# Linear attention and two MLPs on one core: seven block products in place of eight in the second MLP's first layer, and the first MLP two chunks at a time

## The chip, the cores and the metric

The kernel runs on one core of a Trainium2 chip. Times are device microseconds (us); shorter is better. Engines are named as in the profile: PE is TensorE (PEld are its weight loads), DVE VectorE, ACT ScalarE, POOL GpSimd, SP the engine that issues most DMAs.

## The reference

Three parts follow each other. `x` of the attention goes to the first MLP, whose output goes to the second one; `x` has 1152 tokens (2 batches of 576) of 512 features.

```
def phi(x):
    proj = np.einsum('bhsd,df->bhsf', x, w_phi)
    proj = proj - np.max(np.abs(proj), axis=-1, keepdims=True)
    return np.concatenate([np.exp(proj), np.exp(-proj)], axis=-1)
q_p, k_p = (phi(q), phi(k))
num = np.einsum('bhsf,bhfd->bhsd', q_p, np.einsum('bhsf,bhsd->bhfd', k_p, v))
den = np.einsum('bhsf,bhf->bhs', q_p, np.sum(k_p, axis=2))[..., None] + 1e-06
x = (num / den)                     # 2 x 8 heads x 576 x 64, reordered to 1152 x 512
x = (x @ w_a) * (x @ w_b) @ w_out   # 512 -> 1536 -> 512
for e in range(4):                  # p: domain_probs, normed over the 4 experts
    out += p[:, e:e + 1] * (np.maximum(x @ w1[e], 0.0) @ w2[e])   # 512 -> 1024 -> 512
```

## The kernel before

Every value that a matmul of the MLPs reads is held as a high and a low part, each of a rounded 32-bit type (fp32r), and a product of two such values is three matmuls: high weights with high and low data, low weights with high data. High parts are copies on ScalarE, low parts subtractions on VectorE or GpSimd. The weights of the first MLP arrive as 64-bit words (`raw`) and are turned into 32-bit ones on the chip in three stages that lie apart: `words` (two ScalarE operations), `from_words` (three VectorE operations and one addition `wx` on GpSimd, L344) and `parts` (L375, L376).

The attention runs as a pipeline of 36 slots (18 for keys, 18 for queries; `NI` = 36, `NK` = 18) and some slots behind, in which the last divisions are made: `stage_x` on VectorE, and `stage_xparts`, which copies x to its high part (`xh`, L289) and makes the low part (`xl`, L290, GpSimd), a pair of heads at a time, in two pieces, since a batch is 576 tokens and a block 384. In the slots of `FILL` the first products of the first MLP are issued.

In the MLPs all data lie transposed, features on partitions, tokens in columns, in three blocks of 384 tokens (`TB`). Weights stand still in the array, a block's tokens stream. The hidden features come in chunks of 128.

- First MLP: `stage_ab` makes one chunk of one block, `a` and `b` (12 matmuls each), their product `gg` (L417) and its two parts `hh`. `stage_o1` adds the chunk to four tiles of PSUM (`acc`, 12 matmuls); after six chunks (`GF`) these are copied into `part` (L442), and the second six are added to that (L449); the result's two parts (L450, L451) are the second MLP's input.
- Second MLP: `stage_h` makes a chunk of an expert for a block (12 matmuls of 384 columns, L465 to L467), `hh` by relu and a subtraction (L472, L473), `stage_o2` adds it to three row tiles of 128 tokens (9 matmuls of 512 columns, L483 to L485). Per expert and block, eight chunks accumulate in PSUM, then `o2_sum` adds the row tiles, weighed by the tokens' probabilities, to `oacc`.

The order is a list `prog` by hand: the second layer of a chunk is issued after the first layer of the next one. `ahead` splits weights ahead of their use at one half per stage. All engines run their queues in the order of the program.

Of the kernel before, what the change touches and what calls it, by code (L numbers as in the profile page):

```python
# [38 lines left out]

@with_exitstack  # L40
def tile_linear_attention_then_mlps(ctx, tc, qT, kT, v, w_phi, wab, wout, w12, probs, out):
# [6 lines left out]
    wb = const.tile([128, 2, 128], F32, name="wb")  # L48
    wbp = const.tile([128, 2, 256], F32R, name="wbp")
# [4 lines left out]
    w1_p = tc.alloc_tile_pool(name="w1", bufs=1, side="left")  # L54
    k_p = tc.alloc_tile_pool(name="k", bufs=1, side="left")
    r_p = tc.alloc_tile_pool(name="r", bufs=1, side="right")
    q_p = None
    nd_p = tc.alloc_tile_pool(name="nd", bufs=2, space=PSUM)

    with tc.manual_schedule():  # L60
# [4 lines left out]
        # the table of exponentials is loaded while the first inputs are on their way  # L65
# [39 lines left out]
        def load_v(b, st):  # L105
            """Pairs of heads with a block of ones between the two."""
# [85 lines left out]

        def stage_kvz(b, p):
# [5 lines left out]
            t = r_p.tile([128, 2, 2, 128], F32, tag="kvz", name="kvz", bufs=B * NP)  # L199
# [39 lines left out]

        xh, xl = {}, {}  # L240

        def pieces(b):
            lo, end = b * S, (b + 1) * S
            while lo < end:
                tb = lo // TB
                hi = min(end, (tb + 1) * TB)
                yield tb, lo - tb * TB, hi - lo, lo - b * S
                lo = hi

        def stage_num(b, p):  # L250
# [3 lines left out]
            for h in range(2):  # L254
                t = nd_p.tile([128, 2, 512], F32, tag="nd", name="num")
                nd.append(t)
                for i in range(2):
                    for s in range(2):
                        nc.tensor.matmul(
                            out=t[:, i, 0:288], lhsT=kvz[:, h, s, :],  # L260
                            rhs=qp[:, s, h, 288 * i:288 * i + 288],
                            start=(s == 0), stop=(s == 1),
                        )
            den = q_p.tile([128, 2, 288], F32, tag="den", name="den", bufs=2)
            x = q_p.tile([128, 2, 288], F32, tag="x", name="x", bufs=3)
            for h in range(2):
                lo = 64 * h
                nc.scalar.activation(
                    out=den[lo:lo + 64], in_=nd[h][64 - lo:128 - lo, :, 0:288], func=AF.Copy, bias=1e-6
                )  # L270
                nc.scalar.activation(out=x[lo:lo + 64], in_=nd[h][lo:lo + 64, :, 0:288], func=AF.Copy)
            return x, den

        def stage_x(b, p, x, den):
# [5 lines left out]
            rb = q_p.tile([128, 2, 288], F32, tag="rb", name="rb", bufs=1)  # L280
            nc.vector.transpose(out=rb.rearrange("p a b -> p (a b)"), in_=dt.rearrange("p a b -> p (a b)"))
            nc.vector.tensor_tensor(out=x, in0=x, in1=rb, op=ALU.mult)
            return x

        def stage_xparts(b, p, x):
            xf = x.rearrange("p a b -> p (a b)")
            for tb, o, n, s in pieces(b):
                hi = xh[tb][:, p, o:o + n]
                nc.scalar.activation(out=hi, in_=xf[:, s:s + n], func=AF.Copy)  # L289
                nc.gpsimd.tensor_tensor(  # L290
                    out=xl[tb][:, p, o:o + n], in0=xf[:, s:s + n], in1=hi.bitcast(F32), op=ALU.subtract
                )

# [1 line left out]
        w2_p = None  # L295
        w_t = {}
        units = [("ab", f) for f in range(NF)] + [("o", 0), ("ab", 3), ("o", 1), ("ab", 4), ("ab", 5), ("o", 2)]
        units += [u for f in range(GF, FA) for u in [("ab", f)] + ([("o", f // 2)] if f % 2 == 0 else [])]
        units += [("e", n) for n in range(E * FE)]
        srcs = {"ab": wab, "o": wout, "e": w12}  # L300
# [416 lines left out]
```

## Time and profile before

| | |
|---|---|
| runs | 746.52, 746.54, 747.3 us (median 746.54) |
| span of the profiled execution, first to last instruction | 745.0 us, and some 1.5 us around it |
| PE busy | 734.0 us (99%), 3920 matmuls |
| DVE, ACT, POOL busy | 335.4, 268.3, 120.7 us |

The attention takes the first 126 us; then come the first MLP to about 340 us, and the second to 740. "Busy" of PE is the time that any matmul is in flight. A time in a list of instructions is one instruction's own duration; behind it, in brackets, stands how long its engine was idle before, and which instruction ended that.

### The profile page before, as it was taken

To read this page: it belongs to the slowest core of one execution; us is meant where nothing else is said; L and a number is where in the kernel's file an instruction comes from. 1 tells how busy PE (TensorE), PEld (TensorE's weight loads), DVE (VectorE), ACT (ScalarE), POOL (GpSimd) and SP (SyncE) were. 2 spreads that over 40 slices of the span, in tenths; PEclk is the share of its full clock that TensorE was granted. 3 is DMA by queue.
4 is the path that set the end of the run, shared out by engine and by line. 5 is a ranking of instruction groups with operands and counts; after the bars stand their busy time and mean duration, and the time that the engine had idled before them with its cause. 6 is when DMAs were issued, how large, how long until landed. Compare 5 with 4: busy or idle time off the path is not lost.

```text
span 745.0 us, 9704 instructions
## 1 busy us (share of the span) xinstructions
PE 734.0 (99%) x3920; PEld 680.9 (91%) x3920; DVE 335.4 (45%) x553; ACT 268.3 (36%) x546; POOL 120.7 (16%) x114
## 2 busy tenths in 40 slices
PE   7999999999999999999999999999999999999997
PEld 6888889999999999999999898999999899999996
DVE  6987988888179421336122441214332124222131
ACT  5877997566157221334111321112311114121110
POOL 3663436444034120202000000000000000000000
PEclk9999999999999999999999999999999999999999
DMA  7742011344034100023000330001300003001011
GB/s 233 219 129 76 1 38 70 126 163 143 1 107 148 57 0 1 1 86 116 26 1 1 113 113 1 1 0 59 140 29 0 1 16 127 0 1 43 0 44 44
DMA packets 20334, 46.07 MB, mean 62 GB/s; under 512 B 4592, under 2 KB 9136, under 8 KB 20288
## 3 DMA queue, kind: packets, MB, share of 16 engines
q1 hardware_dynamic: 20032, 45.25, 18.4%
q8 instruction: 31, 0.51, 0.3%
q10 hardware_dynamic: 224, 0.16, 0.1%
q14 instruction: 15, 0.12, 0.1%
q0 software_dynamic: 32, 0.03, 0.0%
HBM read 43.08 MB, written 2.36 MB: 61 GB/s over the span
## 4 chain that ended last, share of the span: by engine, by line
PE 87%; DVE 8%; ACT 2%; issue 2%; DMA 0%; DVEq 0%; POOL 0%; POOLq 0%
PE h L465 9%; PE h L467 9%; PE acc L485 9%; PE h L466 9%; PE acc L484 9%; PE acc L483 9%; PE ab L412 5%; PE ab L413 5%; PE ab L411 5%; PE kv L179 4%; PE acc L434 3%; PE acc L435 3%; PE acc L436 3%; DVE m L335 1%; PE pj L148 1%
## 5 line engine op out<-in xcount | busy, mean ns | idle before, releaser
L473 DVE SCALAR_TENSOR_TENSOR hh<-h,hh 128x384 fp32r<-128x384 f32 x96 | 53.6, 559 | 274.6 <-ACT hh L472 274.6
L472 ACT ACTIVATE hh<-h 128x384 fp32r<-128x384 f32 x96 | 47.1, 491 | 310.1 <-PE h L467 310.1
L465 PE MATMUL h<-xh,w 128*128 128x384 f32 x384 | 129.6, 338 | 0.0
L467 PE MATMUL h<-xh,w 128*128 128x384 f32 x384 | 129.6, 338 | 0.0
L466 PE MATMUL h<-xl,w 128*128 128x384 f32 x384 | 128.9, 336 | 0.0
L485 PE MATMUL acc<-w,hh 128*128 128x512 f32 x288 | 114.1, 396 | 0.0
L484 PE MATMUL acc<-w,hh 128*128 128x512 f32 x288 | 113.3, 393 | 0.0
L483 PE MATMUL acc<-w,hh 128*128 128x512 f32 x288 | 113.2, 393 | 0.0
L411 PE MATMUL ab<-xh,w 128*128 128x384 f32 x288 | 96.7, 336 | 0.0
L412 PE MATMUL ab<-xl,w 128*128 128x384 f32 x288 | 96.4, 335 | 0.3 <-POOL xl L290 0.3
L413 PE MATMUL ab<-xh,w 128*128 128x384 f32 x288 | 96.3, 334 | 0.0
L466 PEld LDWEIGHTS h<-xl,w 128*128 128x128 f32 x384 | 72.1, 188 | 3.9
L465 PEld LDWEIGHTS h<-xh,w 128*128 128x128 f32 x384 | 72.1, 188 | 3.8
L467 PEld LDWEIGHTS h<-xh,w 128*128 128x128 f32 x384 | 72.0, 188 | 0.0
L344 POOL TENSOR_TENSOR wx<-wx,rn 128x512 uint32<-128x512 uint32 x36 | 54.6, 1516 | 87.3 <-DVE wx L341 47.0
L485 PEld LDWEIGHTS acc<-w,hh 128*128 128x128 f32 x288 | 54.1, 188 | 12.5
L483 PEld LDWEIGHTS acc<-w,hh 128*128 128x128 f32 x288 | 54.5, 189 | 8.8
L484 PEld LDWEIGHTS acc<-w,hh 128*128 128x128 f32 x288 | 54.1, 188 | 8.9
L412 PEld LDWEIGHTS ab<-xl,w 128*128 128x128 f32 x288 | 54.1, 188 | 0.7 <-POOL xl L290 0.6
L411 PEld LDWEIGHTS ab<-xh,w 128*128 128x128 f32 x288 | 54.1, 188 | 0.1
L413 PEld LDWEIGHTS ab<-xh,w 128*128 128x128 f32 x288 | 54.0, 188 | 0.0
L417 DVE TENSOR_TENSOR gg<-ab,a 128x384 f32<-128x384 f32 x36 | 19.9, 554 | 73.7 <-PE ab L413 72.3
(78 smaller groups left out, 1067.5 us busy)
## 6 DMA issues: line engine op xcount, KB each, us to landing
raw<-in_w SPq DMA_DIRECT2D x32, 512.0 KB, 3.5
raw<-in_wab SPq DMA_DIRECT2D x24, 512.0 KB, 3.6
raw<-in_wout SPq DMA_DIRECT2D x12, 512.0 KB, 3.4
xraw<-in_qT SPq DMA_DIRECT2D x6, 384.0 KB, 3.0
out<-oacc SPq DMA_DIRECT2D x8, 256.0 KB, 2.0
xraw<-in_kT SPq DMA_DIRECT2D x5, 384.0 KB, 3.2
v<-in_v SPq DMA_DIRECT2D x8, 192.0 KB, 3.9
v<-in_v SPq DMA_DIRECT2D x8, 64.0 KB, 3.7
```

Of the source, the lines that this page charges most:

```text
L344: nc.gpsimd.tensor_tensor(out=x, in0=x, in1=r, op=ALU.add)
L411: nc.tensor.matmul(out=t, lhsT=whi, rhs=xh[tb][:, c, :], start=(c == 0), stop=False)
L412: nc.tensor.matmul(out=t, lhsT=whi, rhs=xl[tb][:, c, :], start=False, stop=False)
L413: nc.tensor.matmul(out=t, lhsT=wlo, rhs=xh[tb][:, c, :], start=False, stop=(c == KD - 1))
L465: nc.tensor.matmul(out=t, lhsT=whi, rhs=xh[tb][:, c, :], start=(c == 0), stop=False)
L466: nc.tensor.matmul(out=t, lhsT=whi, rhs=xl[tb][:, c, :], start=False, stop=False)
L467: nc.tensor.matmul(out=t, lhsT=wlo, rhs=xh[tb][:, c, :], start=False, stop=(c == KD - 1))
L472: nc.scalar.activation(out=hh[:, 0, :], in_=t, func=AF.Relu)
L473: nc.vector.scalar_tensor_tensor(out=hh[:, 1, :], in0=t, scalar=0.0, in1=hh[:, 0, :].bitcast(F32), op0=ALU.max, op1=ALU.subtract)
L483: nc.tensor.matmul(out=acc, lhsT=hi, rhs=whi, start=(f == 0), stop=False)
L484: nc.tensor.matmul(out=acc, lhsT=hi, rhs=wlo, start=False, stop=False)
L485: nc.tensor.matmul(out=acc, lhsT=lo, rhs=whi, start=False, stop=(f == FE - 1))
```

## The change

1. The first layer of the second MLP takes two chunks of an expert (256 hidden features, `j`, 16 pairs) and one batch of 576 tokens (`tp`) at a time. Its product is seen as 2 x 2 blocks: 256 of the 512 input features by 128 hidden features on one side, 256 features by 288 tokens (`HT`) on the other. Instead of the eight products of blocks, Strassen's seven are made (in Winograd's form), `M1` to `M7`: each is a sum or difference of weight blocks times one of data blocks, 6 matmuls of 288 columns. Products that are added to each other do so in PSUM (`X`, `Y`, `Z`) or in `c` in SBUF.
2. The sums of weight blocks (`sums_w`, tile `wt`, GpSimd, L409) and their two parts (`wc`), and the differences of data blocks (`sums_x`, tile `t`, GpSimd, L306) and their parts (`xc`, L83 and L84) are new; data are made once for each batch, weights once for each pair of chunks.
3. The second layer of that MLP is done for each pair of chunks and each of nine row tiles (6 matmuls of 512 columns), and each such tile is added to `oacc` at once (L646, L651): 16 x 9 sums where there were 4 x 9.
4. The first MLP takes two chunks and a batch at a time (`unit_ab`: eight steps of 12 matmuls of 288 columns; `o1`: eight pieces of 6 matmuls). The second layer's pieces are added to `part` in SBUF by VectorE (L497) each time.
5. The order comes from a queue: `run` issues a step of the first layer and after it pieces of the second that were queued three or more steps ago, at a rate; `tasks` is the list of the weights' preparations, `prep(1)` issues one of them after each step. Before a hidden tile `hhb`, of which there is now one for a batch, is written again, `free_hh` issues all pieces that read it. The last unit of the first MLP runs its pieces at twice the rate; after the first unit of the second MLP the queue is emptied.
6. x's parts lie by batch and are made in one piece of 576 columns. `FILL` has a slot more, with two steps in each.

The core of the diff, with what is new and called:

```diff
-        xh, xl = {}, {}
-        def pieces(b):
...
         def stage_xparts(b, p, x):
             xf = x.rearrange("p a b -> p (a b)")
-            for tb, o, n, s in pieces(b):
-                hi = xh[tb][:, p, o:o + n]
...
+            hi = xh[b][:, p]
+            nc.scalar.activation(out=hi, in_=xf, func=AF.Copy)
+            nc.gpsimd.tensor_tensor(out=xl[b][:, p], in0=xf, in1=hi.bitcast(F32), op=ALU.subtract)
+        def sums_x(b, a, eng):
+            x = part[b][:, a]
+            t = m_p.tile([128, 4, HT], F32, tag="g", name="t", bufs=3)
+            for o, i, j in ((0, x[:, 0], x[:, 1]), (1, x[:, 2], x[:, 0]), (2, x[:, 2], t[:, 0]), (3, x[:, 3], t[:, 2])):
+                eng.tensor_tensor(out=t[:, o], in0=i, in1=j, op=ALU.subtract)
+            tt[b, a] = t
+        def parts_x(b, a, eng, eng2):
+            x, t = part[b][:, a], tt.pop((b, a))
+            o = xc[b]
+            two_parts(o[:, 0, 0:3, a, :], o[:, 1, 0:3, a, :], x[:, 1:4], eng)
+            two_parts(o[:, 0, 3:7, a, :], o[:, 1, 3:7, a, :], t, eng2)
...
-            t = w1_p.tile([128, 1024], U32, tag="raw", name="raw", bufs=3)
+            t = w_p.tile([128, 1024], U32, tag="raw", name="raw", bufs=2)
...
+        def parts(k):
+            u, f = f64[k]
+            if f == 0:
+                p, n = (w_p, 4) if u[0] == "ab" else (od_p, 2)
+                w_t[u] = p.tile([128, 2, 2, 512], F32R, tag=u[0], name="w", bufs=n)
+            two_parts(w_t[u][:, 0, f], w_t[u][:, 1, f], state.pop(k), nc.gpsimd)
...
+        def sums_w(u):
+            def go():
+                t = stage_t[u]
+                a21, a11, a12, a22, s1, s2, s3, s4 = (t[:, k] for k in range(8))
+                for o, i, j, op in ((s1, a21, a22, ALU.add), (s3, a11, a21, ALU.subtract),
+                                    (s2, s1, a11, ALU.subtract), (s4, a12, s2, ALU.subtract)):
+                    nc.gpsimd.tensor_tensor(out=o, in0=i, in1=j, op=op)
+            return go
+        def parts_w(u, lo, hi):
+            def go():
+                src = stage_t[u]
+                if u[0] == "1":
+                    w_t[u] = wc_t[u[1] % len(wc_t)]
+                    src = src[:, 1:8]
+                elif lo == 0:
+                    w_t[u] = od_p.tile([128, 2, 2, 512], F32R, tag="o", name="w", bufs=2)
+                two_parts(w_t[u][:, 0, lo:hi], w_t[u][:, 1, lo:hi], src[:, lo:hi], nc.gpsimd)
+            return go
...
+        def prep(n):
+            while n > 0 and t_next[0] < len(tasks):
+                u, fn, writes = tasks[t_next[0]]
+                if writes and u in before and uses[before[u]] or t_next[0] >= mark and l_p is None:
+                    return
+                fn()
+                t_next[0] += 1
+                n -= 1
...
+        def product(ps, w, x, m, first):
+            for a in range(2):
+                whi, wlo = (w[:, k, m[0], 128 * a:128 * a + 128] for k in range(2))
+                xhi, xlo = (x[:, k, m[1], a, :] for k in range(2))
+                nc.tensor.matmul(out=ps, lhsT=whi, rhs=xhi, start=first and a == 0, stop=False, skip_group_check=True)
+                nc.tensor.matmul(out=ps, lhsT=whi, rhs=xlo, start=False, stop=False, skip_group_check=True)
+                nc.tensor.matmul(out=ps, lhsT=wlo, rhs=xhi, start=False, stop=a == 1, skip_group_check=True)
...
+        def unit(u, tp, c, row0, half, last):
+            need(u)
+            w, x = w_t[u], xc[tp]
+            lo, hi = slice(0, HT), slice(HT, 2 * HT)
+            X, Y, Z = (u_p.tile([128, HT], F32, tag="u", name=n) for n in ("X", "Y", "Z"))
+            product(X, w, x, M1, True)
+            copy(c[:, 0, hi], X)
+            yield
+            product(Y, w, x, M2, True)
+            add(c[:, 0, hi], Y)
+            yield
+            product(X, w, x, M6, False)
+            copy(c[:, 0, lo], X)
+            yield
+            product(Z, w, x, M5, True)
+            copy(c[:, 1, lo], Z)
+            yield
+            product(X, w, x, M7, False)
+            add(c[:, 1, lo], X)
+            half()
+            yield
+            product(Z, w, x, M3, False)
+            add(c[:, 0, lo], Z)
+            row0()
+            yield
+            product(X, w, x, M4, False)
+            uses[u] -= 1
+            last(X)
+            yield
...
+        def free_hh(tp):
+            n = max([i + 1 for i, q in enumerate(queue) if tp in q[1]], default=0)
+            for _ in range(n):
+                queue.pop(0)[2]()
-        def stage_ab(n):
...
+        def unit_ab(j, tp):
...
+                        if m == 0:
+                            a = p.tile([128, HT], F32, tag="a", name="a", bufs=2)
+                            copy(a, t)
+                        else:
+                            nc.vector.tensor_tensor(out=gg[:, i], in0=t, in1=a, op=ALU.mult)
+                        if (i, m) == (1, 1):
+                            uses[u] -= 1
+                            free_hh(tp)
+                            g = gg.rearrange("p a b -> p (a b)")
+                            copy(hh_of(tp, f, 0), g)
+                            nc.vector.tensor_tensor(
+                                out=hh_of(tp, f, 1), in0=g, in1=hh_of(tp, f, 0).bitcast(F32), op=ALU.subtract
+                            )
+                            if f == 1:
+                                queue.extend(
+                                    (pos[0] + 3, (tp,), lambda d=d, i=i: o1(j, tp, d, i))
+                                    for d in range(KD) for i in range(2)
+                                )
+                        yield
-        def stage_o1(n, hh, acc):
...
+        def o1(j, tp, d, i):
...
+            if j == 0:
+                if d == 0 and i == 0:
+                    part[tp] = m_p.tile([128, 2, 4, HT], F32, tag="pb", name="part", bufs=2)
+                copy(part[tp][:, d // 2, 2 * (d % 2) + i], acc)
+            else:
+                add(part[tp][:, d // 2, 2 * (d % 2) + i], acc)
+            if j == FP1 - 1 and i == 1 and d % 2 == 1:
+                sums_x(tp, d // 2, nc.gpsimd)
+                parts_x(tp, d // 2, nc.vector, nc.vector)
-        def stage_h(n):
...
-        def o2_products(n, hh, acc, i):
...
-        def stage_o2(n, hh, acc):
...
+        def unit_h(j, tp):
+            c = new_c("h")
+            def parts(src, f, lo, hi):
+                free_hh(tp)
+                nc.scalar.activation(out=hh_of(tp, f, 0, lo, hi), in_=src, func=AF.Relu)
+                nc.vector.scalar_tensor_tensor(
+                    out=hh_of(tp, f, 1, lo, hi), in0=src, scalar=0.0, in1=hh_of(tp, f, 0, lo, hi).bitcast(F32),
+                    op0=ALU.max, op1=ALU.subtract,
+                )
+            def last(X):
+                parts(X, 1, HT, 2 * HT)
+                rows = range(4) if tp == 0 else range(4, 9)
+                queue.extend((pos[0] + 3, (0, 1) if i == 4 else (tp,), lambda i=i: o2(j, i)) for i in rows)
+            return unit(
+                ("1", j), tp, c, lambda: parts(c[:, 0], 0, 0, 2 * HT), lambda: parts(c[:, 1, :HT], 1, 0, HT), last
+            )
+        def o2(j, i):
...
+                oc = o[:, c:c + step]
+                nc.vector.scalar_tensor_tensor(
+                    out=oc, in0=acc[:, c:c + step], scalar=sc, in1=oc, op0=ALU.mult, op1=ALU.add
+                )
...
-        prog = g0("a00 a01 a02 a10 a11 a12 a20 a21 a22 o00 o01 a03 o02 a04 o03 a05 o04")
...
+        def run(gen, rate, tasks_per):
+            for _ in gen:
+                pos[0] += 1
+                credit[0] = min(credit[0] + rate, 2.0)
+                while credit[0] >= 1.0 and queue and queue[0][0] <= pos[0]:
+                    queue.pop(0)[2]()
+                    credit[0] -= 1.0
+                prep(tasks_per)
...
-        FILL = [NI + 4, NI + 6, NI + 7]
+        FILL = [NI + 4, NI + 6, NI + 7, NI + 8]
+        fill = unit_ab(0, 0)
...
-        for pos in range(NF, len(prog)):
-            emit(pos)
-            ahead(pos)
...
+        for j in range(FP1):
+            for tp in range(B):
+                run(unit_ab(j, tp) if j + tp else fill, 2.0 if j + 1 == FP1 and tp else 1.0, 1)
...
+        for j in range(FP2):
+            for tp in range(2):
+                run(unit_h(j, tp), 0.7 if j + tp else 1.5, 1)
+                while j + tp == 0 and queue:
+                    queue.pop(0)[2]()
+        while queue:
+            queue.pop(0)[2]()
```

GpSimd's order at the join of the MLPs, first of the kernel before: its last additions of weights (`wx`, 26 in a row), and the low parts of the three blocks' input of the second MLP.

```order
L344 TENSOR_TENSOR wx<-wx,rn 128x512 x26
L451 TENSOR_TENSOR xl<-part,xh 128x384 x12
```

And after, from the first preparation of the second MLP's weights on (`wt` sums and `wc` low parts, `w` parts of the second layer, `t` differences of `part`):

```order
L409 TENSOR_TENSOR wt<-wt 128x256 x4
L84 TENSOR_TENSOR wc<-wt,wc 128x768
L306 TENSOR_TENSOR t<-part 128x288 x2
L306 TENSOR_TENSOR t<-part,t 128x288 x2
L84 TENSOR_TENSOR wc<-wt,wc 128x512 x2
L306 TENSOR_TENSOR t<-part 128x288 x2
L306 TENSOR_TENSOR t<-part,t 128x288 x2
L84 TENSOR_TENSOR w<-wx,w 128x512 x2
```

Where GpSimd had twelve low parts it has differences of `part` in turn with work on weights; two more such groups of four differences, for the second batch, follow with four `wt` sums between them.

VectorE's order at the join, after, from the last batch 0 sums on (rows of the last `ab` unit among them):

```order
L84 TENSOR_TENSOR xc<-part,xc 128x3x288
L84 TENSOR_TENSOR xc<-t,xc 128x4x288
L571 TENSOR_TENSOR gg<-ab,a 128x288 x2
L577 TENSOR_TENSOR hhb<-gg,hhb 128x576
L497 TENSOR_TENSOR h<-Y,h 128x288
L497 TENSOR_TENSOR part<-acc,part 128x288 x4
L84 TENSOR_TENSOR xc<-part,xc 128x3x288
L84 TENSOR_TENSOR xc<-t,xc 128x4x288
L497 TENSOR_TENSOR part<-acc,part 128x288
L497 TENSOR_TENSOR h<-X,h 128x288
```

Here the subtractions for the two batches (3 x 288 = 864 and 4 x 288 = 1152 columns) stand between the last hidden tiles of the first MLP and the first sums of the second, and ahead of the sum that frees `X`.

ScalarE's order at the end of the attention, before (`xh` of the last pair of heads in two pieces):

```order
L415 ACTIVATE a<-ab 128x384
L422 ACTIVATE hh<-gg 128x384
L289 ACTIVATE xh<-x 128x192
L289 ACTIVATE xh<-x 128x384
L415 ACTIVATE a<-ab 128x384
```

And after:

```order
L494 ACTIVATE a<-ab 128x288
L494 ACTIVATE hhb<-gg 128x576
L83 ACTIVATE w<-wx 128x512
L298 ACTIVATE xh<-x 128x576
L494 ACTIVATE a<-ab 128x288 x2
```

The last high part of x is one copy now, and a copy of weights stands ahead of it too.

## Rows read from the trace of the kernel before

**Rows 1.** The page: span, TensorE's busy time, and the chain that ended last, by engine.

```profile
span 745.0 us, 9704 instructions
PE 734.0 (99%) x3920; PEld 680.9 (91%) x3920; DVE 335.4 (45%) x553; ACT 268.3 (36%) x546; POOL 120.7 (16%) x114
...
PE 87%; DVE 8%; ACT 2%; issue 2%; DMA 0%; DVEq 0%; POOL 0%; POOLq 0%
```

**Rows 2.** Waits of ScalarE and TensorE: us in total, times, longest.

```profile
ACT hh L472 <- PE h L467: 310.1, 95, 3.7
...
PE acc L434 <- ACT part L442: 1.0, 1, 1.0
```

**Rows 3.** Stretches: length, busy us and instructions of each engine, clock, DMA.

```profile
20.00:40.00 20.00, 20.00 (x126) 17.72 (x126) 19.05 (x33) 16.64 (x34) 12.81 (x14) 1.00 0.68 203
...
200.00:250.00 50.00, 50.00 (x289) 50.00 (x288) 38.31 (x59) 27.99 (x54) 17.67 (x11) 1.00 0.34 116
...
400.00:450.00 50.00, 50.00 (x252) 45.25 (x251) 20.65 (x34) 14.18 (x28) 0.00 (x0) 1.00 0.26 85
...
700.00:745.00 45.00, 40.82 (x203) 36.34 (x202) 9.57 (x17) 4.42 (x9) 0.00 (x0) 0.98 0.10 36
```

**Rows 4.** TensorE's instructions in the projections, in order of time.

```profile
14.42 0.28 PE L149 MATMUL pj<-wbp,xp 128*128 128x256 f32 x1
14.53 0.28 PE L150 MATMUL pj<-wbp,xp 128*128 128x256 f32 x1
14.65 0.28 PE L148 MATMUL pj<-wbp,xp 128*128 128x256 f32 x1
14.76 0.28 PE L149 MATMUL pj<-wbp,xp 128*128 128x256 f32 x1
14.88 0.27 PE L150 MATMUL pj<-wbp,xp 128*128 128x256 f32 x1
```

**Rows 5.** Groups by line and shape: busy us, mean ns of one, idle before.

```profile
L465 PE MATMUL h<-xh,w 128*128 128x384 f32 x384 | 129.6, 338 | 0.0
...
L376 DVE TENSOR_TENSOR w<-raw,w 128x512 fp32r<-128x512 f32 x64 | 42.7, 707 | 1.1 <-ACT w L375 1.1
...
L71 POOL TENSOR_TENSOR xp<-xraw,xp 128x256 fp32r<-128x256 f32 x33 | 25.3, 777 | 24.8 <-ACT xp L70 23.5 <-PE rt L212 1.4
...
L496 DVE SCALAR_TENSOR_TENSOR oacc<-acc,pr,oacc 128x512 f32<-128x512 f32 x26 | 18.0, 743 | 9.3 <-PE acc L485 9.3
...
L451 POOL TENSOR_TENSOR xl<-part,xh 128x384 fp32r<-128x384 f32 x12 | 12.7, 1101 | 85.5 <-ACT xh L450 85.5
L376 POOL TENSOR_TENSOR w<-wx,w 128x512 fp32r<-128x512 f32 x8 | 12.2, 1524 | 0.0
...
L449 DVE TENSOR_TENSOR part<-acc,part 128x384 f32<-128x384 f32 x12 | 5.8, 548 | 0.0
L450 ACT ACTIVATE xh<-part 128x384 fp32r<-128x384 f32 x12 | 5.8, 525 | 3.5 <-DVE part L449 3.5
```

**Rows 6.** VectorE's L335 and GpSimd's L344 in order of time.

```profile
145.81 0.42 DVE L335 TENSOR_SCALAR m<-m 128x512 f32<-128x512 f32 x1
...
151.68 1.60 POOL L344 TENSOR_TENSOR wx<-wx,rn 128x512 uint32<-128x512 uint32 x1 [2.51 <-ACT w L375]
...
152.05 1.51 DVE L335 TENSOR_SCALAR m<-m 128x512 f32<-128x512 f32 x1
```

**Rows 7.** VectorE and GpSimd at the join of the MLPs, in order of time.

```profile
339.63 1.94 DVE L449 TENSOR_TENSOR part<-acc,part 128x384 f32<-128x384 f32 x4
...
340.81 4.85 POOL L451 TENSOR_TENSOR xl<-part,xh 128x384 fp32r<-128x384 f32 x4 [31.01 <-ACT xh L450]
```

**Rows 8.** The end of the attention, in order of time: VectorE, ScalarE, GpSimd, TensorE.

```profile
120.74 1.83 DVE L282 TENSOR_TENSOR x<-x,rb 128x576 f32<-128x576 f32 x1
...
123.50 0.76 ACT L289 ACTIVATE xh<-x 128x192 fp32r<-128x192 f32 x2
...
123.92 1.69 POOL L290 TENSOR_TENSOR xl<-x,xh 128x192 fp32r<-128x192 f32 x2 [0.20 <-ACT xh L289]
...
124.70 0.44 PE L412 MATMUL ab<-xl,w 128*128 128x384 f32 x1 [0.28 <-POOL xl L290]
```

More of the change, by code (lines that the diff above doesn't have):

```diff
@@ L295, in tile_linear_attention_then_mlps @@
-        w2_p = None
-        w_t = {}
[L297 to L300, printed above, removed]
-        halves = [(i, j) for i in range(len(units)) for j in range(2)]
-        raws = {}
-        loads = [(i, j) for i, j in halves if units[i][0] != "e" or j == 0]
@@ L382, in need @@
-        def need(u):
-            while u not in w_t:
-                if nxt["split"] <= 2 * units.index(u) + 1:
-                    split_half(nc.vector)
-                elif begun:
-                    middle()
-                else:
-                    parts(nc.vector)
-        part = {}
-        def early_hh(later_on):
-            if later_on:
-                return gb_p.tile([128, 2, TB], F32R, tag="hh0", name="hh0", bufs=2 * NF)
-            return g_p.tile([128, 2, TB], F32R, tag="hh0", name="hh0", bufs=NF)
@@ L561, in emit @@
[L561 to L573 removed]
+            state[k] = x.bitcast(F32)
@@ new lines, in tile_linear_attention_then_mlps @@
+        tasks = []
+        NW = len(f64)
+        for k in range(NW + 2):
+            if k >= 2:
+                tasks.append((f64[k - 2][0], lambda k=k: parts(k - 2), f64[k - 2][1] == 0))
+            if 1 <= k <= NW:
+                tasks.append((f64[k - 1][0], lambda k=k: middle(k - 1), False))
+            if k < NW:
+                tasks.append((f64[k][0], lambda k=k: begin(k), False))
+        late = units[3 * FP1:]
+        tasks += [(late[i], load_w(late[i]), True) for i in range(2)]
@@ new lines, in need @@
+        def need(u):
+            last = max(i for i, t in enumerate(tasks) if t[0] == u)
+            if t_next[0] <= last:
+                prep(last + 1 - t_next[0])
+                assert t_next[0] > last, u
+        pos = [0]
+        queue = []
+        credit = [0.0]
+        hhb = [None]
+        part = {}
+        oacc = {}
+        acc_p = None
+        def product(ps, w, x, m, first):
[5 more added lines that the diff above has]
+                nc.tensor.matmul(out=ps, lhsT=wlo, rhs=xhi, start=False, stop=a == 1, skip_group_check=True)
@@ new lines, in nothing, with new_c, hh_of @@
+        def nothing():
+            pass
+        def new_c(name):
+            return m_p.tile([128, 2, 2 * HT], F32, tag="g", name=name, bufs=3)
+        def hh_of(tp, f, k, lo=0, hi=2 * HT):
+            if hhb[0] is None:
+                assert not qp_t and len(kvz_t) == B * NP
+                hhb[0] = hh_p.tile([128, 2, 2, NT], F32R, tag="hh", name="hhb")
+            return hhb[0][:, f, k, 2 * HT * tp + lo:2 * HT * tp + hi]
+        def free_hh(tp):
+            n = max([i + 1 for i, q in enumerate(queue) if tp in q[1]], default=0)
+            for _ in range(n):
+                queue.pop(0)[2]()
@@ L648, in tile_linear_attention_then_mlps @@
             if slot in FILL:
[L649 to L651 removed]
+                for _ in range(2):
+                    next(fill)
+                    pos[0] += 1
+            if 4 <= slot < NK - 1 and slot % 2 == 0:
+                prep(3)
+            if slot >= NI:
+                prep(1)
         assert not todo
```

409 lines of the change are left out of this document (163 added, 246 removed).

## The prediction

> **What bounds the kernel now.** I read the page first. TensorE is busy for 734.0 of the 745.0 us and 87% of the chain that ended last is its own [rows 1]. The waits say the same from the other side: ScalarE's copy of a hidden tile (L472) waited 310.1 us for TensorE, while TensorE's longest wait inside the MLPs is 1.0 us, for the copies of `part` (L442) [rows 2]. So a matmul less is time less, and work on the other engines is free until TensorE waits for it. How much slack they have is in the table by stretches [rows 3]: in the second MLP (400 to 450 us) TensorE is full, VectorE has 20.65 of 50 us, ScalarE 14.18, GpSimd nothing.
>
> The same table gives the price of a matmul. A matmul's own duration (338 ns, [rows 5]) is no price, since they are pipelined; the spacing is. 200 to 250 us holds 289 matmuls of 384 columns in 50.0 us of full TensorE: 0.173 us each. 400 to 450 us holds 252: 12 rounds, each of one chunk and one block of tokens, with 12 matmuls of 384 and 9 of 512 columns. A round is 4.167 us, and a 512-column matmul (4.167 - 12 x 0.1733) / 9 = 0.232. Where 256 columns stream, in the projections, the starts go from 14.42 to 14.88 in four steps: 0.115 each [rows 4]. That is 0.450, 0.451 and 0.453 ns per column: no fixed part. 288 columns occur nowhere; between 256 and 384 on this line they cost 0.130 (bounds: 0.115, the price of 256, and 0.173, the price of 384).
>
> **The change, part by part.** *Products removed.* The first layer of the second MLP has 1152 matmuls of 384 columns (3 x 384, [rows 5]). Seven products of 6 matmuls, for 16 pairs of chunks and 2 batches, are 1344 of 288. 1152 x 0.1733 = 199.6 us become 1344 x 0.130 = 174.7: **-24.9 us**. The second layer keeps its 864 matmuls of 512. The first MLP becomes 1152 + 576 matmuls of 288 where it had 864 + 432 of 384, with equal columns: 0. At the upper bound of 0.173 all of these together would cost +33 + 75, at the lower -45 - 26; three rows on one line leave neither much weight.
>
> [...]
>
> *The join of the two MLPs.* Before, the adds, copies and low parts of a block (4 x L449 in 1.94 us, 4 x L451 in 4.85 us) ran under the next products of the other blocks, and TensorE did not wait [rows 7]. Now the seven operands of a batch come from all of its `part`: GpSimd makes four differences per half batch (L306), ScalarE copies 864 and 1152 columns per partition (L83), VectorE subtracts them (L84), and the last unit of the first MLP stands right ahead. Prices scaled by columns from [rows 5]: VectorE 288 from PSUM 0.455 (0.548 at 384), SBUF 576 0.80, 864 1.07, 1152 1.37 (0.707 at 512, about 0.2 of it fixed); ScalarE 288 0.41, 576 0.68, 864 0.92, 1152 1.16 (0.525 at 384); GpSimd 288 0.85 (0.777 at 256, 1.101 at 384) and 512 1.52. I walked the new order of four engines with these, and TensorE waits five times:
> 1. First products (`M1`, `M2`): they need banks of PSUM that the last `ab` tiles leave. The copy of the last `a` stands on ScalarE behind `xc<-t`, which needs four GpSimd differences: 0.46 + 3.4 + 1.16 + 0.41 + 0.46 and handoffs = 6.1 behind the last sum, of which two steps of `ab`, 2 x 12 x 0.130, cover 3.1: 3.0, and 0.5 more for GpSimd's backlog: 3.5.
> 2. The first `o1` of the last unit: two subtractions of 864 and 1152 (2.4) stand on VectorE ahead of `gg`, then the copy and the subtraction of 576 (1.5) follow; less two products (1.6): 2.2.
> 3. `M4`: the add that frees its bank is queued behind the two subtractions for batch 1, which wait for four differences behind `wt` and `w` work on GpSimd: 4.4.
> 4. Row 0 of `o2`: relu and subtraction of 576 behind the last `Z`: 2.2.
> 5. Row 2 of `o2`: the relu of `X` stands on ScalarE behind the two copies for batch 1's second half and a copy of 768: 3.5.
> Sum **+16 us**. Low end 8 (half of the queueing is met by work I priced too high), high end 22 (GpSimd and VectorE hold each other, below).
>
> *The end of attention.* The last low part of x was made in two instructions, 1.69 us from 123.92; TensorE waited 0.28 and went on at 124.70, when the first of them had landed [rows 8]. The work that fills this wait has the same columns as before (72 x 384, 96 x 288). Now a single instruction of 576 columns does it all; it stands on GpSimd behind a low part of weights, and its high part on ScalarE behind `a`, `hhb` and `w`. From the same start of the division (x ends at 122.5) I get 0.68 for the copy, some 1 of queueing and 1.7 for the low part, so 126.4. **+2 us**, 0 to 4.
>
> *Splitting during attention.* One `begin`, two `parts` and one `middle` more stand at 20 to 57 us, where VectorE is busy 19.05 of 20 us [rows 3], and two raw buffers stand in for three: **+0.5**, 0 to 3. The copies of `part` that held TensorE for 1.0 us [rows 2] become one add per tile: **-1**. Inside the first MLP, a step is 12 + 6 matmuls, 2.34 us, and asks on average for some 1.5 us of the fullest engine: 0, up to 4.
>
> *Steady state of the second MLP.* A pair of chunks takes 84 x 0.130 + 54 x 0.232 = 23.4 us of TensorE. VectorE per pair: 6 adds and 4 subtractions at 0.455, 2 subtractions of 576 at 0.80, 9 sums at 0.743 = 12.8; ScalarE about 8.6; GpSimd 4 x 0.777 + 2.3 + 4 x 1.524 = 11.5. None is full. The tight place is from batch 1's last product to the row of `o2` that needs both batches: add, relu, subtraction, add, relu of 576 and subtraction of 576 make 0.46 + 0.44 + 0.46 + 0.46 + 0.68 + 0.80 and handoffs = 3.6 against about 5.0 of products. It leaves about 1.2: I take **0**. If cover is gone, each of the 15 such places costs what it overruns.
>
> What is unpriced there is GpSimd's work beside VectorE's. A VectorE `m` (L335) takes 0.42 us alone, and 1.51 when GpSimd's add (L344, 1.60) began just before it [rows 6]: it waits for the end of GpSimd's instruction. [...]
>
> **Sum.** 746.5 - 24.9 + 16 + 2 + 0.5 - 1 = 739.1; about 0.4 for the tail, where the last row waits for its subtraction of 576, gives **739.5**. The profiled execution's span is 745.0, 1.5 below the median of the runs; the terms are differences, so they are laid on the median.
>
> **The rivals.** *The join is hidden* (0.24): the waits 1 to 5 hold 5 us or less, because GpSimd gets through its differences while TensorE still has products. 746.5 - 24.9 + 5 + 2 = 729. For it: VectorE and ScalarE are half idle; against it: the queue order, in which copies stand behind things that are late.
> *Held at every pair* (0.12), the one on the other side: VectorE's subtractions wait for GpSimd's low parts at each of the 15 places where batch 1 ends. With slack 1.2 us and two waits of up to 1.5, a place overruns by 0 to 1.8; at 1.5, +22.5, so 762. It decides from (746.5 - 739.5) / 15 = 0.5 us per place. For it: [rows 6]; against it: GpSimd's share is half, and its slots are spread over the seven steps.
> *Weight loads bind* (0.02): a matmul of 288 columns costs what one of 384 does: 1344 x 0.173 instead of 199.6, and 1728 x 0.173 instead of 224.6, so 746.5 + 33 + 75 = 855. Against it: [rows 4], where 256-column matmuls with a load each pass every 0.115 us.
> *A lower clock* (0.04): the granted clock is 1.00 in every full stretch and 0.98 only in the last, with the idle end [rows 3]. Waits of 4 us at the join could cost 2 to 6 us: 744. No row shows a gap of that size in the MLPs. That the change does nothing is no case: TensorE's rows are counted and fewer columns stand there.
>
> **How the numbers follow.** The forecast, 733 to 747, gets 0.58; the others as above. The range for 8 in 10 takes in the hidden join from 728.5 and the forecast with its high ends up to 752 (a join of 22, attention 4, a place 0.3 over). Runs of this kernel differ by up to 0.8 us, so 0.2% (1.5 us) is about what can be told from no change: that is 745.0 to 748.0. Faster: hidden 0.24, most of the forecast 0.52, half the clock case 0.02, 0.78 in all; same: 0.05 of the forecast and the other half of the clock case, 0.07; slower: held 0.12, loads 0.02, and 0.01 of the forecast's upper end, 0.15.
>
> **What would show it right or wrong.** 288-column matmuls at 0.130 in full stretches, so 23.4 us per pair of chunks in the second MLP; a spacing above 0.14 fails the first term. At the join, TensorE's waits for the `xc`, `hhb` and `h` lines, with 16 us in all. At the end of attention, a wait for `xl` (L299). In the second MLP no wait longer than 0.3 us; a repeated wait for `hhb` L614 at each pair is the rival. VectorE instructions of L614 of twice their shortest time would show the holding.

## The result

| | before | after |
|---|---|---|
| median of 4 runs | 746.53 us | 739.75 us (739.59 to 741.05) |
| ratio to the kernel before, 95% interval | | 0.9911, 0.9897 to 0.9925 |
| profiled execution: time, span | span 745.0 | 739.64, span 737.7 |

The forecast was 739.5. The page of the changed kernel begins so (busy us, share of the span, instructions; then the chain that ended last, by engine):

```profile
span 737.7 us, 11553 instructions
PE 718.8 (97%) x4544; PEld 662.0 (90%) x4544; DVE 428.0 (58%) x741; ACT 322.6 (44%) x650; POOL 310.3 (42%) x282
...
PE 81%; DVE 8%; ACT 4%; DMA 3%; POOL 2%; issue 2%; SPq 0%; DVEq 0%; POOLq 0%; ACTq 0%
```

TensorE has 624 matmuls more and is busy 15 us less, GpSimd works 310 us where it worked 121, and the chain, 87% TensorE in [rows 1], now passes through the other engines more often. TensorE's longest waits behind the start of the program (us in total, times, longest):

```profile
PE X L489 <- DVE h L497: 2.4, 1, 2.4
PE acc L635 <- ACT hhb L613: 1.7, 3, 0.8
PE Y L489 <- ACT a L494: 1.5, 1, 1.5
PE pj L161 <- DVE r L168: 1.4, 2, 1.0
PE acc L594 <- ACT hhb L494: 1.1, 1, 1.1
PE acc L595 <- DVE hhb L577: 0.7, 2, 0.4
```

All but `pj`, and one of the two of `hhb L577`, lie between 337 and 374 us, at the join of the two MLPs. The stretches (length, busy us and instructions of each engine, clock, DMA):

```profile
340.00:345.00 5.00, 3.53 (x25) 3.08 (x24) 3.28 (x7) 1.55 (x4) 1.28 (x1) 1.00 0.72 222
345.00:350.00 5.00, 5.00 (x40) 5.00 (x39) 2.07 (x3) 2.23 (x4) 3.96 (x5) 1.00 0.02 4
350.00:355.00 5.00, 2.57 (x18) 2.34 (x17) 2.59 (x5) 1.61 (x2) 4.92 (x5) 0.97 0.00 0
355.00:360.00 5.00, 4.25 (x12) 3.21 (x12) 3.26 (x7) 1.61 (x2) 2.72 (x5) 0.50 0.01 2
360.00:365.00 5.00, 4.22 (x14) 2.78 (x13) 3.11 (x5) 2.71 (x4) 2.99 (x2) 0.85 0.00 0
...
500.00:550.00 50.00, 50.00 (x294) 45.12 (x293) 26.71 (x46) 17.49 (x36) 19.87 (x18) 1.00 0.14 43
```

The last row stands beside the one of 400 to 450 us in [rows 3]: TensorE is full in both, with VectorE at 27 instead of 21 us and GpSimd at 20 instead of 0. The steady second MLP has no wait. From 355 to 360 us the clock is 0.50, and matmuls of 288 columns start 0.24 to 0.26 us apart and those of 512 some 0.43, where they started 0.13 and 0.23 apart at 1.00. The matmuls that run slowly, 6 of 288 and 11 of 512 columns, begin with the first of these rows, behind the longest wait, and end at the second:

```profile
354.50 0.46 PE L489 MATMUL X<-xc,wc 128*128 128x288 f32 x1 [2.43 <-DVE h L497]
...
361.67 0.39 PE L637 MATMUL acc<-w,hhb 128*128 128x512 f32 x1
```

**The size of the steady gain** is read from starts of TensorE's instructions. Before: 12 chunks of the first MLP (36 matmuls each) between the first two rows, 48 rounds of the second between the last two.

```profile
247.71 0.34 PE L411 MATMUL ab<-xh,w 128*128 128x384 f32 x1
...
323.07 0.34 PE L411 MATMUL ab<-xh,w 128*128 128x384 f32 x1
...
436.41 0.34 PE L465 MATMUL h<-xh,w 128*128 128x384 f32 x1
...
638.01 0.34 PE L465 MATMUL h<-xh,w 128*128 128x384 f32 x1
```

After: 9 units of the first MLP (144 matmuls each), 8 pairs of chunks of the second.

```profile
146.13 0.29 PE L564 MATMUL ab<-xh,w 128*128 128x288 f32 x1
...
317.96 0.29 PE L564 MATMUL ab<-xh,w 128*128 128x288 f32 x1
...
444.14 0.29 PE L489 MATMUL Y<-xc,wc 128*128 128x288 f32 x1
...
632.96 0.29 PE L489 MATMUL Y<-xc,wc 128*128 128x288 f32 x1
```

Second MLP: a round was 201.60 / 48 = 4.200 us, 96 rounds 403.2; a pair is 188.82 / 8 = 23.60, 16 pairs 377.6: **-25.6 us**. First MLP: 75.36 / 432 = 0.1744 us per matmul of 384 columns, 1296 are 226.1; 171.83 / 1296 = 0.1326 per one of 288, 1728 are 229.1: **+3.0 us**.

### The profile page after: what moved, and what is told of

Read it like the earlier page. It is cut to its first block, busy times and chain, and to the rows that moved or that the text cites. A ratio compares the mean times of both kernels' runs of the same rounds, so it can differ in the third digit from the quotient of the medians.

```text
span 737.7 us, 11553 instructions
## 1 busy us (share of the span) xinstructions
PE 718.8 (97%) x4544; PEld 662.0 (90%) x4544; DVE 428.0 (58%) x741; ACT 322.6 (44%) x650; POOL 310.3 (42%) x282
## 4 chain that ended last, share of the span: by engine, by line
PE 81%; DVE 8%; ACT 4%; DMA 3%; POOL 2%; issue 2%; SPq 0%; DVEq 0%; POOLq 0%; ACTq 0%
PE acc L637 9%; PE acc L636 9%; PE acc L635 9%; PE ab L566 6%; PE ab L564 6%; PE ab L565 6%; PE X L490 4%; PE X L489 4%; PE X L491 4%; PE num L270 3%; PE acc L595 3%; PE acc L596 3%; PE acc L594 3%; PE Z L489 2%; PE Z L490 2%; PE Z L491 2%
## 5 line engine op out<-in xcount | busy, mean ns | idle before, releaser
L84 POOL TENSOR_TENSOR w<-wx,w 128x512 fp32r<-128x512 f32 x68 | 88.7, 1312 | 229.3 <-ACT w L83 229.3
L651 DVE SCALAR_TENSOR_TENSOR oacc<-acc,pr,oacc 128x512 f32<-128x512 f32 (+1 forms) x136 | 101.1, 744 | 110.3 <-PE acc L637 110.3
L635 PE MATMUL acc<-w,hhb 128*128 128x512 f32 x288 | 114.1, 396 | 1.7 <-ACT hhb L613 1.7
L637 PE MATMUL acc<-w,hhb 128*128 128x512 f32 x288 | 114.2, 396 | 0.2
L636 PE MATMUL acc<-w,hhb 128*128 128x512 f32 x288 | 114.2, 396 | 0.0
L564 PE MATMUL ab<-xh,w 128*128 128x288 f32 x384 | 113.5, 296 | 0.0
L566 PE MATMUL ab<-xh,w 128*128 128x288 f32 x384 | 113.1, 295 | 0.0
L565 PE MATMUL ab<-xl,w 128*128 128x288 f32 x384 | 113.0, 294 | 0.0
L84 POOL TENSOR_TENSOR wc<-wt,wc 128x512 fp32r<-128x512 f32 (+1 forms) x48 | 73.7, 1539 | 34.3 <-ACT wc L83 34.3
L613 ACT ACTIVATE hhb<-h 128x288 fp32r<-128x288 f32 x64 | 36.2, 565 | 99.4 <-DVE h L497 99.4
L489 PE MATMUL X<-xc,wc 128*128 128x288 f32 x256 | 75.9, 297 | 2.4 <-DVE h L497 2.4
L490 PE MATMUL X<-xc,wc 128*128 128x288 f32 x256 | 75.9, 296 | 0.0
L491 PE MATMUL X<-xc,wc 128*128 128x288 f32 x256 | 75.6, 295 | 0.0
L637 PEld LDWEIGHTS acc<-w,hhb 128*128 128x128 f32 x288 | 54.6, 189 | 13.8 <-DVE hhb L614 1.7
L614 DVE SCALAR_TENSOR_TENSOR hhb<-h,hhb 128x288 fp32r<-128x288 f32 x64 | 40.8, 637 | 42.2 <-ACT hhb L613 42.2
L635 PEld LDWEIGHTS acc<-w,hhb 128*128 128x128 f32 x288 | 54.6, 189 | 10.0 <-ACT hhb L613 2.7
L636 PEld LDWEIGHTS acc<-w,hhb 128*128 128x128 f32 x288 | 54.6, 190 | 7.3
```

The lines of the kernel that those rows point to most:

```text
L84: eng.tensor_tensor(out=lo, in0=src, in1=hi.bitcast(F32), op=ALU.subtract)
L489: nc.tensor.matmul(out=ps, lhsT=whi, rhs=xhi, start=first and a == 0, stop=False, skip_group_check=True)
L490: nc.tensor.matmul(out=ps, lhsT=whi, rhs=xlo, start=False, stop=False, skip_group_check=True)
L491: nc.tensor.matmul(out=ps, lhsT=wlo, rhs=xhi, start=False, stop=a == 1, skip_group_check=True)
L564: nc.tensor.matmul(out=t, lhsT=whi, rhs=hi, start=(c == 0), stop=False)
L565: nc.tensor.matmul(out=t, lhsT=whi, rhs=lo, start=False, stop=False)
```

## The experiments

Each was timed in turn with the kernel before; ratios are to that. The changed kernel has 0.9911.

**The join: order or data.** The copies and subtractions of batch 1's `xc` wait until the first unit is over:

```diff
-                parts_x(tp, d // 2, nc.vector, nc.vector)
+                if tp == 0:
+                    parts_x(tp, d // 2, nc.vector, nc.vector)
+                else:
+                    deferred.append(lambda: parts_x(tp, d // 2, nc.vector, nc.vector))
...
+        deferred = []
...
                 run(unit_h(j, tp), 0.7 if j + tp else 1.5, 1)
+                while j + tp == 0 and deferred:
+                    deferred.pop(0)()
```

> The copies and subtractions that make batch 1's xc are issued behind the first unit of the second MLP, not among its steps. Theory (queue order): TensorE's 2.4 us before M4 and the two 0.8 us waits of the o2 rows come from VectorE and ScalarE work that stands behind batch 1's late differences, and the clock of 0.73 at 350 to 360 us from these waits, so both go: 739.7 becomes 730 to 734, with at most 2 us of a new wait ahead of the second unit. Rival (late data): the same waits only move to the second unit's first products: 737 to 741.

Measured 736.35 us, ratio 0.9854 (0.984 to 0.9869): 4.3 us less, between the two. TensorE's waits in the join (330 to 400 us):

```profile
PE X L490 <- DVE xc L84: 1.7, 2, 1.0
PE Y L489 <- ACT a L494: 1.5, 1, 1.5
PE acc L594 <- ACT hhb L494: 1.1, 1, 1.1
PE X L489 <- DVE h L497: 0.4, 1, 0.4
...
PE acc L640 <- ACT hhb L618: 0.3, 1, 0.3
```

By their places in the trace, the last two lines and the first are waits of the second unit. In the first unit nothing is left of the 2.4 us before `M4` and of the rows' waits, so these came from the queues; in the second unit 2.2 us are new, 1.7 of them for `xc`. And the clock, which I had put down to the wait before `M4`, fell earlier in this profile:

```profile
340.00:345.00 5.00, 3.52 (x16) 3.07 (x15) 2.86 (x7) 1.50 (x3) 1.28 (x1) 0.76 0.61 186
345.00:350.00 5.00, 5.00 (x36) 5.00 (x36) 1.38 (x3) 1.34 (x3) 3.02 (x4) 0.90 0.00 0
```

**The clock.** First, four added products ahead of `M4`:

```diff
+            if u == ("1", 0) and tp == 0:
+                fl = acc_p.tile([128, HT], F32, tag="acc", name="acc")
+                for n in range(4):
+                    product(fl, w, x, M1, True)
             product(X, w, x, M4, False)
```

> 24 matmuls of 288 columns whose result nobody reads are issued ahead of M4 in the first unit of the second MLP; they are added work and fill the wait of 2.4 us there. Theory (clock by idling): about 5 of the 12 us lost at the join are matmuls at half clock after that wait, so with the wait filled the clock stays at 1.00 and the time falls by 4 to 5 us less the 0.7 us by which the added work is longer than the wait: 735 to 737. Rival (the clock falls for the many short waits before, or for none of them): added work costs what it is over the wait, 739.5 to 741.

740.52 us, 0.991 (0.9893 to 0.9927), no gain, but it told nothing: the added work itself waited for its bank of PSUM behind the same VectorE subtractions.

```profile
PE acc L489 <- DVE part L497: 2.1, 1, 2.1
```

Then, on top of the deferred `xc`, added products where banks were free:

```diff
+            if u == ("1", 0) and tp == 0:
+                fl = acc_p.tile([128, HT], F32, tag="acc", name="fill")
+                for n in range(2):
+                    product(fl, w, x, M1, True)
             product(Y, w, x, M2, True)
+            if u == ("1", 0) and tp == 0:
+                for n in range(2):
+                    product(fl, w, x, M1, True)
```

> As e1, and 12 matmuls of 288 columns whose result nobody reads ahead of M2 and 12 behind it, in a bank of PSUM that nothing else waits for, where TensorE waited 1.5 and 1.1 + 0.4 us; each lot is 1.6 us of added work. Theory (clock by idling): in e1 the clock fell to 0.76 at 340 to 345 us and 0.90 at 345 to 350, some 2 to 4 us of matmuls at half clock, right behind these waits; with TensorE busy it stays at 1.00 there, and the time falls by 2 to 3 us against e1, to 733 to 734 where e1 has 736. Rival (the clock has another cause): 736 to 737, the added work not being free.

734.36 us, 0.983 (0.9813 to 0.9848), 1.8 us under the deferred one, with 24 matmuls more. The two intervals overlap by 0.0008, but the highest run here (734.79) lies under the lowest there (735.94). The clock stays up where it had fallen:

```profile
340.00:345.00 5.00, 4.85 (x37) 4.62 (x36) 2.94 (x7) 1.87 (x5) 1.29 (x1) 1.00 0.66 204
345.00:350.00 5.00, 5.00 (x40) 5.00 (x40) 2.20 (x5) 1.42 (x4) 4.28 (x5) 1.00 0.02 3
```

Last, without the deferring: the same 24, and 18 more matmuls into the bank of `Y` ahead of `M4`.

```diff
+            if u == ("1", 0) and tp == 0:
+                for n in range(3):
+                    product(Y, w, x, M1, True)
             product(X, w, x, M4, False)
```

> The changed kernel with added matmuls alone, in the places where TensorE waited in the first unit of the second MLP, and in banks that nothing else waits for: 12 ahead of M2, 12 behind it, 18 ahead of M4 (5.6 us of work that nobody reads against 5.4 us of waits there). What e2 was to tell. Theory (clock by idling): TensorE is busy to M4, the clock stays at 1.00 to 355 us, and the matmuls behind run at full rate: 735 to 737, against 739.7. Rival (the clock does not hang on these waits): 739.5 to 741.

739.96 us, 0.9904 (0.9889 to 0.9919): no gain. The wait at `M4` is gone and the clock is 1.00 up to 360 us, but TensorE waits that much longer behind it, 4.1 us for `hhb` where it was 1.7, and behind the longest of these waits the clock falls after all:

```profile
PE acc L645 <- ACT hhb L623: 4.1, 3, 2.6
...
360.00:365.00 5.00, 2.61 (x7) 1.81 (x8) 3.66 (x5) 2.71 (x4) 2.99 (x3) 0.80 0.00 0
365.00:370.00 5.00, 5.00 (x32) 4.72 (x31) 1.25 (x3) 1.96 (x5) 1.92 (x3) 0.86 0.00 0
```

The first matmul of row 2 of `o2`, in the changed kernel and then here:

```profile
363.52 0.50 PE L635 MATMUL acc<-w,hhb 128*128 128x512 f32 x1 [0.78 <-ACT hhb L613]
```

```profile
362.39 0.50 PE L645 MATMUL acc<-w,hhb 128*128 128x512 f32 x1 [2.57 <-ACT hhb L623]
```

The last `ab` started at 336.93 in the changed kernel and at 335.75 here, so row 2 comes 26.6 us behind it in both (row 0 20.0 in both). Up to there the clock of 0.50 of the changed kernel cost nothing: it ran while TensorE would have waited for `hhb` behind batch 1's `xc`. What the clock at 1.00 would be worth behind row 2 this run does not tell. Where this chain was out of the way, in the run before, keeping the clock was worth 1.8 us. These runs speak for a clock that hangs on TensorE's waits, 0.76 at 340 to 345 us behind the waits of the deferred kernel and 1.00 with the same waits filled, though not in every execution: the profile of the changed kernel has 1.00 behind the same waits (340 to 350 us).

**Batch 0 a unit earlier**, on top of the deferred `xc`:

```diff
+        ab_units = [(j, tp) for j in range(FP1) for tp in range(B)]
+        ab_units[-3:] = [(FP1 - 1, 0), (FP1 - 2, 1), (FP1 - 1, 1)]
```

> As e1, and the last three units of the first MLP run in the order pair 5 batch 0, pair 4 batch 1, pair 5 batch 1, so that batch 0's part is whole a unit (19 us) earlier. Theory (the copy of the last a stands behind batch 0's late xc on ScalarE): TensorE's wait ahead of M2 (1.5 us) goes, and that of the first o1 (1.1 + 0.4) shrinks, as nothing of batch 0's xc is left on VectorE ahead of gg: 2 us off e1, and 2 to 3 more if the clock then does not fall: 731 to 734. Rival (hidden tiles are late by themselves, or weights come too late in the new order): 736 or more.

750.99 us, 1.0053 (1.0034 to 1.0072): a miss. The last pair's weights are wanted a unit earlier and are not split yet:

```profile
PE ab L564 <- ACT w L83: 6.5, 3, 3.3
...
PE acc L594 <- ACT w L83: 2.2, 1, 2.2
```

The wait ahead of `M2` is gone, as expected, but the price lies in the splitting of weights, which has less than a unit to spare.

**The attention: the probabilities.**

```diff
-            if slot == 16:
-                probabilities()
...
         assert not todo
+        probabilities()
```

> The four VectorE operations on the experts' probabilities, with their load, are moved from slot 16 of the attention to behind it. Theory (VectorE's queue in the last slots of the keys): these hold 1.6 us of waiting for the load and 1.3 us of waiting for GpSimd, and the attention's projections fall 2.3 us behind there; without them the first matmul of the first MLP comes 2 us earlier, 737 to 738.5. Rival (two raw buffers and the added split of weights delay the attention): no change, 739 to 740.

737.51 us, 0.9873 (0.9857 to 0.989): 2.8 us less than the changed kernel. The first matmul of the first MLP came at 109.67 in the changed kernel and comes at 107.10 here, in the profiles (one row of each, in this order):

```profile
109.67 0.51 PE L564 MATMUL ab<-xh,w 128*128 128x288 f32 x1
```

```profile
107.10 0.51 PE L564 MATMUL ab<-xh,w 128*128 128x288 f32 x1
```

That is one execution of each. In the eight profiles with the probabilities in slot 16 the first `ab` starts between 108.49 and 109.67 us, in the three with them behind the attention (two are of experiments further down) between 106.81 and 107.69. What stood in slot 16 of the changed kernel (VectorE, then GpSimd, then TensorE):

```profile
52.05 0.19 DVE L694 TENSOR_REDUCE psm<-pr 128x9 f32<-128x36 f32 x1 [1.58 <-DMA pr<-in_probs]
52.27 1.27 DVE L695 TENSOR_SCALAR psm<-psm 128x9 f32<-128x9 f32 x1
...
52.24 1.28 POOL L84 TENSOR_TENSOR w<-wx,w 128x512 fp32r<-128x512 f32 x1 [1.25 <-ACT w L83]
...
57.08 0.36 PE L161 MATMUL pj<-wbp,xp 128*128 128x256 f32 x1 [1.01 <-DVE r L168]
```

A VectorE operation on nine columns takes 1.27 us, as long as GpSimd's low part that began with it. In the kernel before, VectorE waits for the load too, but the same operation is short:

```profile
48.21 0.19 DVE L594 TENSOR_REDUCE psm<-pr 128x9 f32<-128x36 f32 x1 [1.33 <-DMA pr<-in_probs]
48.44 0.17 DVE L595 TENSOR_SCALAR psm<-psm 128x9 f32<-128x9 f32 x1
```

The experiment moves the load and the operations together; what each is worth alone is not shown.

**Two raw buffers, in the kernel before.**

```diff
-            t = w1_p.tile([128, 1024], U32, tag="raw", name="raw", bufs=3)
+            t = w1_p.tile([128, 1024], U32, tag="raw", name="raw", bufs=2)
...
-                for _ in range(3):
+                for _ in range(2):
                     load_raw()
```

> The kernel before with two raw buffers, and two loads ahead, where it had three. Theory (VectorE's queue and the probabilities' place made the attention later, not the buffers): no change, 746.5 to 747.5. Rival (the buffers): 1 us or more later, 748 to 750.

761.26 us, 1.0192 (1.0176 to 1.0208). The time is far off either expectation, but the attention, which was the question, is not later: its first `ab` starts at 105.55, and in the kernel before at 105.88 (first row):

```profile
105.88 0.55 PE L411 MATMUL ab<-xh,w 128*128 128x384 f32 x1
```

```profile
105.55 0.55 PE L411 MATMUL ab<-xh,w 128*128 128x384 f32 x1
```

The loss lies in the first MLP, where the old scheme lives on its lead of buffers:

```profile
PE acc L434 <- ACT part L442: 5.3, 2, 3.9
...
PE acc L434 <- ACT hh L422: 4.6, 4, 1.4
```

**GpSimd's work doubled**, each sum of weight blocks made twice:

```diff
-                    nc.gpsimd.tensor_tensor(out=o, in0=i, in1=j, op=op)
+                    for _ in range(2):
+                        nc.gpsimd.tensor_tensor(out=o, in0=i, in1=j, op=op)
```

> The four GpSimd sums of weight blocks of each pair of chunks are made twice, 3 to 4 us more of GpSimd in each 23.6 us. Theory (slack): TensorE has no wait in the second MLP's steady stretches, so GpSimd and VectorE have room: 739 to 741. Rival (VectorE is held behind GpSimd and the slack is nearly gone): waits for hhb at each of the 15 boundaries of 0.3 us or more, 744 or more.

742.98 us, 0.9948 (0.9932 to 0.9964): 2.8 us more, but all of it at the join, in waits and in matmuls at a lower clock (0.64 at 340 to 345 us, 0.67 at 345 to 350):

```profile
PE acc L636 <- ACT hhb L614: 4.5, 3, 3.0
...
500.00:550.00 50.00, 50.00 (x293) 44.96 (x292) 26.65 (x44) 16.93 (x35) 26.76 (x26) 1.00 0.16 47
```

From 400 to 720 us there is no wait even with GpSimd at 27 of 50 us. The waits of VectorE for GpSimd do occur, but are few. In the changed kernel, VectorE's low part of 288 columns took 1.23 us just after the join, until 0.3 us behind the end of two low parts of GpSimd (2.54 us from 369.62), but it is the only one of 32 held so long: their mean is 0.48 us, and that of the 32 with 576 columns 0.79 (in the last two rows: count, busy us, mean ns):

```profile
371.25 1.23 DVE L614 SCALAR_TENSOR_TENSOR hhb<-h,hhb 128x288 fp32r<-128x288 f32 x1 [0.51 <-ACT hhb L613]
...
L614 DVE SCALAR_TENSOR_TENSOR hhb<-h,hhb 128x576 fp32r<-128x576 f32 x32 | 25.3, 792 | 25.8 <-ACT hhb L613 25.8
L614 DVE SCALAR_TENSOR_TENSOR hhb<-h,hhb 128x288 fp32r<-128x288 f32 x32 | 15.4, 483 | 16.4 <-ACT hhb L613 16.4
```

**An eighth product** in each unit, whose result nobody reads:

```diff
+            fl = acc_p.tile([128, HT], F32, tag="acc", name="acc")
+            product(fl, w, x, M1, True)
             product(Z, w, x, M3, False)
```

> An eighth product of 6 matmuls of 288 columns, whose result nobody reads, in each of the 32 units of the second MLP. Theory (price by columns): 192 more matmuls at 0.132 are 25.4 us, 765; so that with eight products the rest of the change costs 18 us over the kernel before. Rival (part of the 23.6 us per pair is the other engines' pace): less than 20 us more, under 760.

763.59 us, 1.0223 (1.0206 to 1.0239), so 0.0312 x 746.5 = 23.3 us for 192 matmuls, 0.121 each, near the 25.4 of the theory. In the steady stretch a pair of chunks takes 25.20 us here instead of 23.60, so its 12 added matmuls cost 0.133 each, as the rows of the changed kernel say; the 12 of the first pair stand in a stretch with waits. With eight products the change would be slower by 2%.

**All together.** The deferred `xc`, the filled waits and the late probabilities:

> e5 with the probabilities behind the attention as in e3: xc of batch 1 behind the first unit, waits ahead of M2 and the first o1 filled, four VectorE operations moved. If the two places are independent the gains add up: e5 stands at 0.983 of the kernel before, e3 took 0.0038 off, so 0.979, 731 to 732. Rival (an earlier attention only waits longer at the join, or the clock falls elsewhere): 733 to 735.

732.34 us, 0.9807 (0.9791 to 0.9823), between the two expectations and nearer the first: the gains add up, but for some 1 us. And with GpSimd's sums for the second pair held back until the first unit is over:

```diff
+                if quiet and u == ("1", 1) and tasks[t_next[0] - 1][0] == ("2", 1):
+                    return
                 fn()
...
+                quiet[:] = [1] if j + tp == 0 else []
                 run(unit_h(j, tp), 0.7 if j + tp else 1.5, 1)
```

> As e10, and GpSimd's four sums of weights for the second pair of chunks, 4 us, are held back until the first unit of the second MLP is over. Theory (GpSimd's queue makes batch 1's differences late): TensorE's 1.7 us of waits for xc ahead of the second unit shrink by 1 us or more, 730 to 731. Rival (VectorE's and ScalarE's parts of xc are what is late): the same as e10, 731 to 732.

730.86 us, 0.9785 (0.9771 to 0.98), under both kernels: 15.9 us less than before. Its four runs all lie under those of the kernel without the holding back. The waits for `xc` are gone, and of the join 0.7 us of waits are left, most of them this one:

```profile
PE acc L650 <- ACT hhb L628: 0.5, 1, 0.5
```

## Why the prediction held, and where it did not

- **Seven products for eight: right.** -24.9 forecast, -25.6 measured; the eighth product costs 23.3 us when it is put back, and 16 x 1.60 = 25.6 by the steady pairs. The two prices were each 1% low (4.167 and 23.4 us against 4.200 and 23.60), since I counted matmuls in a stretch of 50 us, where one more or less is 0.4%; their difference hardly suffers.
- **The first MLP at 0: wrong by 3.0 us.** Equal columns are not quite equal time: 0.1326 against 0.1744 is 0.460 against 0.454 ns per column. My three-point line had no room for that.
- **The join at +16: right in its places, too large in its sum.** All five waits stand where I had put them: 1.5, 1.1 + 0.4, 2.4, 0.8 and 0.8 us, 7.1 with the next of 0.2, against 15.8. The term left out was the clock: the 55 us behind the last `ab` hold 198 matmuls of 288 columns and 71 of 512, at 0.1326 and 0.232 us 42.7 us of work, so 12.3 are lost, and 5.2 of them are not waits. Some 3 of these are slow matmuls: the 17 from 354.50 us on, 3.35 us of work at these prices that took 6.4 besides the wait of 0.8 among them. The other 2 lie next to the waits and are no matter of the clock: the kernel with all three experiments, at 1.00 throughout the join, loses 2.0 beyond its waits too. In the expectations above I had taken about 5 us for the clock. A lower clock was a rival of small chance; it came along with the forecast, and the rows' waits were smaller because of it, as the filled kernel shows. The 2 to 6 us that I gave that rival for waits of 4 us were a guess of mine that no row of the kernel before shows; here the slow matmuls came behind a wait of 2.4 us and cost some 3.
- **The attention at +2.5: right in size, wrong in place.** The first `ab` starts 3.8 us later than in the profile of before, 2.6 to 3.8 by the eight profiles. I put +2 on the last `xl` and 0.5 on the splitting; the terms given for `xl` end at 125.9 us and not at 126.4, so +1.2. TensorE never waits for `xl`, and most of the loss, 2.3 us, arises in the last slots of the keys, where moving the probabilities brings back 2.6 in the profile. That two raw buffers are not the cause is shown for the kernel before alone; of the changed one no run has three. What the remaining 1.2 us are stays open. The -1 for the copies of `part` came: that wait is gone.
- **No waits in the steady second MLP: right.** The rival of held VectorE is refuted here: from 374 us on TensorE never waits, and with 7 us more of GpSimd in 50 us it does not from 400 us on. The sign that I had named, an L614 of twice its shortest time, occurs once, at 371 us, and costs no wait in the steady part. The `m` of [rows 6] reads one tile, the subtractions of that rival read two, and that these are held too it did not show; the L614 of 1.23 us does. The weight-load rival fell with the 0.1326 us spacing.

Sum of the terms as measured: -25.6 + 3.0 + 12.3 + 3.8 - 1 = -7.5, beside -7.3 between the spans of the two profiles from which the terms come, and -6.8 between the medians. The forecast's nearness to the time owes something to errors of opposite sign: the join 3.7 too dear, the first MLP and the attention 4.3 too cheap.

## What to carry to other kernels

Where one engine is full, fewer streamed columns are worth their spacing (here 0.1326 us for 288 and 0.1744 for 384), and spacing is read between starts that lie many periods apart. A change of this kind is paid for at its seams: list what each engine's queue holds there, and put work that is needed later behind work that is waited for now. Filling waits with idle matmuls kept the clock here (1.00 instead of 0.76 at 340 to 345 us), but gained only where no other chain set the pace: 1.8 us on top of the deferred `xc`, nothing alone.

## What was not expected of the hardware

With TensorE's waits of 1.5, 1.1 and 0.4 us and matmuls between them, the mean clock of 340 to 350 us was 0.83 in the profiles of the deferred `xc` and of the late probabilities, and 1.00 in the profile of the changed kernel. A VectorE operation of 0.17 us (in the kernel before) took 1.27 beside a GpSimd operation of 1.28 that started with it. Such an operation and a wait of 1.6 us for a load, in a place without slack, were together worth 2.8 us when moved; in the kernel before a wait of 1.3 us for the same load had cost TensorE nothing.
